# Attention with a row filter and a mixture of experts: a row index moved to the scalar engine, a small copy moved to GpSimd, and second buffers for finished rows

## The chip, the cores and the metric

The kernel runs on one core of a Trainium2 chip. The metric is the device time of one execution in microseconds (us), lower is better. The core's engines run their own instruction queues in order and meet through semaphores: the tensor engine (PE; its weight loads are PEld), the vector engine (DVE), the scalar engine (ACT), GpSimd (POOL) and the sync engine (SP), which only issues DMAs here. POOL issues the indirect DMAs, those whose row addresses lie in a tile.

## The reference

Eight batches of eight heads, 576 rows, head width 64, all float32. Attention keeps, for each row, the scores that reach its 32nd largest; the result is the input of a mixture of eight experts in which each of the 4608 tokens goes to the expert of its largest logit.

```python
scores = scale * np.matmul(q, k.transpose(0, 1, 3, 2))
kth = np.partition(scores, -top_k, axis=-1)[..., -top_k:-top_k + 1]
scores = np.where(scores >= kth, scores, -1000000000.0)
attn = np.exp(scores - np.max(scores, axis=-1, keepdims=True))
x = (attn / (np.sum(attn, axis=-1, keepdims=True) + 1e-09)) @ v     # then [B*S, H*D]
logits = x @ w_gate; expert_idx = np.argmax(logits, axis=1)
out[mask] = gate_w[mask, None] * (np.maximum(x[mask] @ w1[e], 0.0) @ w2[e])
```

## The kernel before

**Steps and batches.** The attention part is one Python loop over 144 steps `t` (18 to a batch, 9 to a group `n` of four heads). A step owns a pair of 128-row score tiles. In the instruction order of step `t` stand: on ACT the exponential of step t-4 (`exps`, L451), the signs of step t-2 (`softmax`, L429) and the copies of the scores of step t+3 out of PSUM (L356, L375); on PE the score matmuls of t+3 (L354), the products with v of step t-5 (L460), the transposes of step t-3 (L446); on POOL the masking of step t-2 (L430) and the small tile `nb` of step t-1 (L990); on DVE the search for the 32 largest of step t (`topk`: 21 maxima over chunks, L988, then rounds of maxima and replacements, L994). Seven pairs of score tiles rotate, so an engine can run some steps ahead of another.

**Jobs.** All other work is written as Python generators (`j_...`) that advance between steps. A `yield need(...)` ends a segment and says what the next one needs; `advance` runs at most one segment of each job after a step, as long as its sums of needs stay under `LIMITS`. What a segment puts in the POOL queue is issued at once behind the step (`gq`); what it puts in the PE, ACT and DVE queues (`pq`, `aq`, `dq`) is issued inside the next step, the DVE part between the instructions of L994. All of these have line L252 in the profile. After the 144 steps `advance` is called without limits, and then in `drain`, one round between two pieces of the expert part.

- `j_rows(n)` scales the finished rows into `xm`, `xl` and the parts of their logits into `lp`, `lpl` (DVE), and SP stores these.
- `j_find(b)` finds up to 128 rows of batch b whose filter has to be done again. It makes their numbers `li` (copied by ACT from PSUM), joins both columns to an index `fl`, and lets POOL gather by it: `r_at`, `r_nb`, a segment later `r_sb`.
- `j_redo(b)` filters these rows anew; it begins when `j_find(b)` has ended (`FOUND`), and starts `j_patch(b)`, whose first segment may run only at positions 1 to 5 of a group of nine (`FREE`), as long as steps last.
- `j_route(b)` finds the expert of each token. `hist` holds a running count in column `KB` and the batch's one-hot columns behind it; a windowed sum gives `cum`, whose last column is the new running count. It is read by the next batch's sum, and by a matmul in two batches and once at the end.

**Expert part.** Weights come in pieces, are split in two parts by ACT, DVE and POOL (L919 to L922), and feed three matmuls for each product (L1107, L1122). Five smaller units of work on tokens of early batches begin before all tokens are routed; their rows are gathered by POOL (`gx`, L841), three gathers just ahead of their transposes (L1087).

Of the kernel before, what the change touches and what calls it, by code (L numbers as in the profile page):

```python
# [8 lines left out]
F32 = mybir.dt.float32  # L9
F32R = mybir.dt.float32r  # L10
BF = mybir.dt.bfloat16
I32 = mybir.dt.int32
I8 = mybir.dt.int8
AF = mybir.ActivationFunctionType
OP = mybir.AluOpType
# [32 lines left out]
def attention_moe(ctx, tc, q, k, v, w_gate, w1, w2, out):  # L48
# [214 lines left out]
    def need(**k):  # L263
        return k
# [249 lines left out]
    def j_rows(n):  # L514
        b = 2 * n // HP

        xm = jobs.tile([128, 2 * MAIN, 128], F32, name="xm", bufs=1)
        xl = jobs.tile([128, 128], F32, name="xl", bufs=1)
        lp = jobs.tile([128, 2 * MAIN, 2 * E], F32, name="lp", bufs=1)
        ll_ = jobs.tile([128, 2 * E], F32, name="lpl", bufs=1)  # L520
        pts = {}

        def turned(m):
            pt = pts[m] = bank()
            for c in range(3 * m, min(3 * m + 3, 2 * MAIN)):
                i, g = divmod(c, 2)
                pe(nc.tensor.matmul, pt[:, (c - 3 * m) * RW:(c - 3 * m + 1) * RW], XT[2 * n + g][:, i * 128:(i + 1) * 128],
                   turner[:, (2 * n + g) % HP], start=True, stop=True)

        def scaled(x, l, pt, r):  # L530
            w = pt.shape[1] // RW
            v = pt.rearrange("p (c x) -> p c x", x=RW)
            vec(nc.vector.tensor_tensor, x.rearrange("p c (h d) -> p c h d", h=2),
                v[:, :, 0:128].rearrange("p c (h d) -> p c h d", h=2), r.to_broadcast([128, w, 2, D]), op=OP.mult)
            vec(nc.vector.tensor_tensor, l.rearrange("p c (h e) -> p c h e", h=2),
                v[:, :, 128:].rearrange("p c (h e) -> p c h e", h=2), r.to_broadcast([128, w, 2, E]), op=OP.mult)

        def done(m):
            c = slice(3 * m, min(3 * m + 3, 2 * MAIN))
            w = c.stop - c.start  # L540
            r = RI[n][0].rearrange("p i g h -> p (i g) h")[:, c, :, None]
            scaled(xm[:, c], lp[:, c], pts[m][:, 0:w * RW], r)

        yield need(bank=1, pe=0.75)
        turned(0)
        while n not in RI:
            yield
        for m in range(2):
            yield need(bank=1, pe=0.75 if m == 0 else 1.1, dve=0.6)
            done(m)  # L550
            vec(release, pts[m])
            turned(m + 1)
        pt = pts[2]
        o = 2 * RW
        for g in range(2):
            r = slice(g * LEFT, (g + 1) * LEFT)
            pe(nc.tensor.matmul, pt[r, o:o + RW], XT[2 * n + g][:, 512:S], turner[:, (2 * n + g) % HP], start=True, stop=True)
        for h in range(2):
            for g in range(2):
                r = slice(g * LEFT, (g + 1) * LEFT)  # L560
                pe(nc.tensor.matmul, pt[r, o + RW + h:o + RW + h + 1], ident[:, h * LEFT:(h + 1) * LEFT],
                   RI[n][1][:, g:g + 1], start=True, stop=True)
        yield need(dve=1.0)
        done(2)
        rl = jobs.tile([128, 2], F32, name="rl")
        vec(nc.vector.tensor_copy, rl, pt[:, o + RW:o + RW + 2])
        scaled(xl[:, None], ll_[:, None], pt[:, o:o + RW], rl[:, None, :, None])
        vec(release, pt)
        yield
        yield  # L570
        t0 = PAD + b * S
        for dst, x, l in ((xs, xm, xl), (lps, lp, ll_)):
            w = dst.shape[1] // 4
            f = slice((n % 2) * 2 * w, (n % 2 + 1) * 2 * w)
            nc.sync.dma_start(dst[t0:t0 + M, f].rearrange("(p i) f -> p i f", p=128),
                              x.rearrange("p (i g) f -> p i (g f)", g=2))
            for g in range(2):
                nc.sync.dma_start(dst[t0 + M:t0 + S, f.start + g * w:f.start + (g + 1) * w], l[g * LEFT:(g + 1) * LEFT])
        STORED.add(n)
# [8 lines left out]
    def j_find(b):  # L588
        sm = lambda name, shape, dt=F32: jobs.tile(shape, dt, name=name, bufs=1)
        yield need(dve=0.3)  # L590
        key = sm("r_key", [128, NLT])
        vec(nc.vector.scalar_tensor_tensor, key, CNT[b], float(2 * TOPK - S), idx1, op0=OP.not_equal, op1=OP.mult)
        vec(nc.vector.max, rhs[:, :, 0], key)
        ok = sm("r_ok", [128, 9], BF)
        vec(nc.vector.tensor_scalar, ok[:, 0:8], rhs[:, :, 0], 0.0, None, op0=OP.is_gt, op1=OP.add,
            accum_out=ok[:, 8:9])
        nbb = NBB[b % 2]
        ntab = dram.tile([128 * (NLT + 1), 2], F32, name=f"ntab{b}")
        nc.sync.dma_start(ntab.rearrange("(p t) a -> p t a", p=128), nbb)
        yield need(spot=1, pe=0.1)  # L600
        pr, leave = spot("stat")
        pe(nc.tensor.matmul, pr[:, 0:1], before, ok[:, 8:9], start=True, stop=True)
        pe(nc.tensor.matmul, pr[:, 1:3], ones, ok[:, 7:9], start=True, stop=True)
        act(nc.scalar.activation, stat[:, b], pr[:, 0:3], AF.Copy)
        act(leave)
        yield need(slack=1)
        yield need(dve=1.3)
        sl = sm("r_sl", [128, 8], BF)
        vec(nc.vector.scalar_tensor_tensor, sl, slots[:, 0:8], stat[:, b, 0:1], ok[:, 0:8], op0=OP.add, op1=OP.mult)
        oh = sm("r_qx", [128, 512]).bitcast(BF).rearrange("p (j x) -> p j x", j=8)  # L610
        vec(nc.vector.tensor_tensor, oh, slots[:, None, :].to_broadcast([128, 8, 128]),
            sl[:, :, None].to_broadcast([128, 8, 128]), op=OP.is_equal)
        yield need(spot=1, pe=0.5)
        pl, leave = spot("li")
        for j in range(8):
            pe(nc.tensor.matmul, pl[:, 0:2], oh[:, j], rhs[:, j], start=(j == 0), stop=(j == 7))
        li = sm("r_li", [128, 2])
        act(nc.scalar.activation, li, pl[:, 0:2], AF.Copy)
        act(leave)
        yield need(slack=1)  # L620
        yield need(dve=0.1)
        fl = sm("r_fl", [128, 1], I32)
        vec(nc.vector.scalar_tensor_tensor, fl, li[:, 1:2], float(NLT + 1), li[:, 0:1], op0=OP.mult, op1=OP.add)
        yield need(pool=2.0)
        at = sm("r_at", [128, 4], I32)
        pool(nc.gpsimd.indirect_dma_start, out=at, out_offset=None, in_=atab,
             in_offset=bass.IndirectOffsetOnAxis(ap=fl[:, 0:1], axis=0))
        nb = jobs.tile([128, 8], F32, name="r_nb", bufs=3)
        pool(nc.gpsimd.indirect_dma_start, out=nb[:, 0:2], out_offset=None, in_=ntab,
             in_offset=bass.IndirectOffsetOnAxis(ap=fl[:, 0:1], axis=0))  # L630
        yield need(pool=1.8)
        qi = jobs.tile([128, 2], I32, name="r_qi", bufs=3)
        pool(nc.gpsimd.tensor_scalar, qi, at[:, 0:3:2], b * H * S, None, op0=OP.add)
        sb = jobs.tile([128, S], F32, name="r_sb", bufs=2)
        pool(nc.gpsimd.indirect_dma_start, out=sb, out_offset=None, in_=SCD[b],
             in_offset=bass.IndirectOffsetOnAxis(ap=at[:, 0:1], axis=0))
        hf = sm("r_hf", [128, 1])
        pool(nc.gpsimd.tensor_copy, hf, at[:, 1:2])
        hm = jobs.tile([128, H], F32, name="r_hm", bufs=3)
        pool(nc.gpsimd.tensor_scalar, hm, eight, hf, None, op0=OP.is_equal)  # L640
        hmb = hm[:, :, None].to_broadcast([128, H, D])
        pool(nc.gpsimd.tensor_scalar, used[:, b:b + 1], hf, float(H), None, op0=OP.is_lt)
        yield need(pool=0.7)

        low = nb[:, 2:3]
        pool(nc.gpsimd.tensor_scalar, nb[:, 3:4], nb[:, 1:2], 1.0 + 2.0 ** -10, None, op0=OP.mult)
        pool(nc.gpsimd.tensor_scalar, low, nb[:, 0:1], -(2.0 ** -7), None, op0=OP.mult)
        pool(nc.gpsimd.tensor_tensor, low, low, nb[:, 3:4], op=OP.add)
        FOUND[b] = (sb, nb, qi, hmb)
# [106 lines left out]
    def j_route(b):  # L756
# [26 lines left out]
        vec(nc.vector.tensor_tensor, hist[:, :, KB + 1:].rearrange("p e c -> p c e"), oh, valid, op=OP.mult)  # L783
        win = bass.AP(hist.tensor, hist.offset, [list(hist.ap[0]), list(hist.ap[1]), [1, KB + 1], [1, KB + 1]])
        vec(nc.vector.tensor_reduce, cum, win, axis=AX.X, op=OP.add)
        vec(nc.vector.tensor_copy, hist[:, :, KB], cum[:, :, KB])
        yield need(spot=1, pe=0.1, act=0.2)
        act(nc.scalar.activation, ex, sh, AF.Exp)
        rk, leave = spot("rank")
# [5 lines left out]
        act(leave)  # L795
        yield need(slack=1)
        yield need(dve=0.7)
        sm = small("gsm", [128, KB])
        pool(nc.gpsimd.iota, pay[:, :, 3:4], pattern=[[0, KB], [0, 1]], base=0, channel_multiplier=0)
        pos = small("pos", [128, KB], I32)  # L800
# [641 lines left out]
```

## Time and profile before

| | |
|---|---|
| median of 3 runs | 1323.11 us (1320.73 to 1324.79) |
| the profiled execution: its own time, its span | 1327.61 us, 1325.8 us |
| granted clock of the tensor engine, mean | 0.985 |
| busy share of the span: PE, DVE, ACT, POOL | 95%, 78%, 62%, 68% |
| the chain that ended last, by engine | PE 62%, DVE 19%, issue 6%, POOL 5%, ACT 5% |
| attention steps | about 12 to 790 us, a batch about 98 us from the third on |
| 1100 to 1200 us (expert part): PE, DVE busy | 100.00, 37.83 us |

A busy share says how long an engine executed anything, held-up instructions included. The chain is followed back from the last instruction, at each step to what released it or to the instruction before it on its engine; "issue" is time for which the profile shows no cause. Times in a timeline are start, then duration.

### The profile page before, as it was taken

What the parts mean: (1) busy time and instruction counts of PE and PEld (TensorE: products, weight loads), DVE (VectorE), ACT (ScalarE), POOL (GpSimd) and SP (SyncE); (2) the same over time, 40 slices, a digit from 0 to 9 for tenths busy, and PEclk for the clock granted to TensorE, in tenths of its full rate; (3) what the DMA queues carried; (4) which work ended last, traced back from release to release, by engine and by line L of the source; (5) the groups of instructions that cost most, each with busy time, mean ns of one, the idle gap of its engine ahead of it and who ended that gap; (6) DMA issues with size and microseconds to landing.
All of it is one profiled execution on the core that took longest, in us unless ns stands there. A gap on an engine that the chain in (4) does not pass through costs nothing.

```text
span 1325.8 us, 32793 instructions
## 1 busy us (share of the span) xinstructions
PE 1265.1 (95%) x9688; PEld 1007.6 (76%) x9688; DVE 1037.6 (78%) x6838; ACT 823.2 (62%) x1691; POOL 905.2 (68%) x1272
## 2 busy tenths in 40 slices
PE   5999999999999999999999988998999999999997
PEld 3677777777677777777676767888799898989996
DVE  6999999999999999999998985745673333345664
ACT  3998898888788788788887863433233323233442
POOL 3777886887887887888877886754654333245654
PEclk8999999999999999999999997999999999999999
DMA  6656564664655655555654434735654333246774
GB/s 169 202 161 175 172 206 142 174 187 147 174 173 162 169 166 161 170 167 162 173 164 134 150 119 113 221 91 159 157 178 154 109 109 115 88 151 189 219 218 124
DMA packets 271244, 211.25 MB, mean 159 GB/s; under 512 B 136216, under 2 KB 214216, under 8 KB 271056
## 3 DMA queue, kind: packets, MB, share of 16 engines
q1 hardware_dynamic: 260320, 185.92, 48.3%
q0 software_dynamic: 9504, 22.86, 5.4%
q8 instruction: 78, 1.28, 0.4%
q14 instruction: 110, 0.90, 0.2%
q10 hardware_dynamic: 1232, 0.30, 0.1%
HBM read 102.49 MB, written 107.90 MB: 159 GB/s over the span
## 4 chain that ended last, share of the span: by engine, by line
PE 62%; DVE 19%; issue 6%; POOL 5%; ACT 5%; DMA 2%; SPq 1%; POOLq 0%; ACTq 0%; DVEq 0%
PE ph L1107 16%; PE y L1122 15%; DVE cand L988 9%; PE ps L354 6%; PE px L460 6%; PE pt L252 5%; PE tt L446 5%; DVE cand L994 3%; DVE vq L994 3%; PE tt L443 3%; PE px L475 2%; ACT sg L429 2%; POOL sb L430 2%; PE mt L1087 1%; PE px L367 1%
## 5 line engine op out<-in xcount | busy, mean ns | idle before, releaser
L430 POOL TENSOR_TENSOR sb<-sb,sg 128x576 f32<-128x576 f32 x288 | 369.8, 1292 | 133.8 <-ACT sg L429 131.1
L988 DVE MAX8 cand<-sb 128x8 f32<-128x52 f32 (+2 forms) x3024 | 368.9, 211 | 2.8 <-ACT sb L356 2.2
L922 POOL TENSOR_TENSOR wl<-r,wh 128x512 fp32r<-128x512 f32 x110 | 142.4, 1296 | 221.2 <-DVE wh L921 211.8
L429 ACT ACTIVATE sg<-sb,nb 128x576 int8<-128x576 f32 x288 | 223.1, 775 | 23.6 <-POOL nb L990 21.5
L460 PEld LDWEIGHTS px<-et,rv 128*64 128x64 f32 x2688 | 132.1, 138 | 122.6 <-issue 57.5
L1108 ACT ACTIVATE hh<-ph 128x320 fp32r<-128x320 f32 (+3 forms) x136 | 58.3, 428 | 240.8 <-PE ph L1107 218.1
L994 DVE MAX8 vq<-cand 128x8 f32<-128x22 f32 (+7 forms) x1152 | 205.2, 207 | 0.8 <-DVE cand L994 0.8
L451 ACT ACTIVATE et<-tt 128x1152 f32<-128x1152 f32 x144 | 163.1, 1132 | 44.3 <-PE tt L446 43.5
L354 PE MATMUL ps<-qk 64*128 64x512 f32 (+1 forms) x576 | 183.9, 646 | 3.1 <-ACT sb L356 2.5
L1109 DVE SCALAR_TENSOR_TENSOR hl<-ph,hh 128x320 fp32r<-128x320 f32 (+3 forms) x136 | 65.1, 479 | 149.9 <-ACT hh L1108 128.9
L460 PE MATMUL px<-et,rv 128*64 128x128 f32 (+1 forms) x2688 | 166.7, 268 | 14.8 <-ACT xt L252 4.7
L356 ACT ACTIVATE sb<-ps 128x1024 f32<-128x1024 f32 x144 | 147.0, 1020 | 51.1 <-PE ps L354 48.1
L1107 PE MATMUL ph<-xh,wh 128*128 128x320 f32 (+3 forms) x536 | 168.3, 314 | 0.0
L446 PE MATMUL tt<-turner,sb 128*128 128x128 f32 x1296 | 166.5, 273 | 0.6 <-POOL sb L430 0.6
L1107 PE MATMUL ph<-xh,wl 128*128 128x320 f32 (+3 forms) x536 | 165.0, 308 | 0.0
L1107 PE MATMUL ph<-xl,wh 128*128 128x320 f32 (+3 forms) x536 | 164.7, 307 | 0.0
L994 DVE MATCH_REPLACE8 cand<-vq,cand 128x22 f32<-128x22 f32 (+2 forms) x864 | 157.8, 190 | 0.0
L446 PEld LDWEIGHTS tt<-turner,sb 128*128 128x128 f32 x1296 | 139.4, 141 | 1.0 <-POOL sb L430 1.0
L1122 PE MATMUL y<-wh,hh 128*128 128x512 f32 x324 | 128.2, 396 | 1.3 <-ACT yo L1126 1.3
L1122 PE MATMUL y<-wh,hl 128*128 128x512 f32 x324 | 128.4, 396 | 0.0
L1122 PE MATMUL y<-wl,hh 128*128 128x512 f32 x324 | 128.2, 396 | 0.0
L1107 PEld LDWEIGHTS ph<-xh,wh 128*128 128x128 f32 x536 | 101.2, 189 | 3.5 <-issue 0.6
(245 smaller groups left out, 2398.2 us busy)
## 6 DMA issues: line engine op xcount, KB each, us to landing
r<-in_moe_w_dram SPq DMA_DIRECT2D x220, 256.0 KB
sc<-sb SPq DMA_DIRECT2D x128, 288.0 KB
sc<-sb SPq DMA_DIRECT2D x128, 256.0 KB
rv<-in_v_dram SPq DMA_DIRECT2D x32, 256.0 KB
xs<-xm SPq DMA_DIRECT2D x16, 512.0 KB
rq<-in_q_dram SPq DMA_DIRECT2D x60, 128.0 KB
rk<-in_k_dram SPq DMA_DIRECT2D x60, 128.0 KB
sc<-sb SPq DMA_DIRECT2D x32, 144.0 KB
```

The lines of the kernel that those rows point to most:

```text
L354: nc.tensor.matmul(MAINS[:, n], qk[:, 0, w], qk[:, 1, 2 * LEFT:], start=True, stop=True)
L356: nc.scalar.activation(bass.AP(EX[-1].tensor, EX[-1].offset, [list(EX[-1].ap[0]), [S + LEFT, 2], [1, M]]), MAINS, AF.Copy)
L429: nc.scalar.activation(upper(SG[i]), SB[u], AF.Sign, bias=nb[:, i, 1:2], accum_out=CNT[b][:, 2 * lt + i:2 * lt + i + 1])
L430: nc.gpsimd.tensor_tensor(SB[u], SB[u], SG[i], op=OP.add)
L446: nc.tensor.matmul(tt[:, c], x[:, c * 128:(c + 1) * 128], ident, start=False, stop=c in (3, 7, 8), is_transpose=True)
L451: nc.scalar.activation(ET[t], three.rearrange("p (c q) -> p c q", c=NB9), AF.Exp, scale=0.125)
L460: yield lambda kb=kb, blk=blk: nc.tensor.matmul(px[h * 64:(h + 1) * 64], block(rv, p % 2, kb if kb < MAIN else MAIN + n, h), et[:, blk, q] ...
L922: (nc.gpsimd if i else nc.vector).tensor_tensor(lo, r, hi, op=OP.subtract)
L988: one[m][0](*one[m][1])
L994: f(*a)
L1107: nc.tensor.matmul(ph, a[:, c, :], x[:, c, s], start=(m == 0), stop=(m == len(seq) - 1))
L1122: nc.tensor.matmul(PY[u, t], a[:, s], x, start=(f == 0 and m == 0), stop=(f == FC - 1 and m == 2))
```

## The change

`xm`, `xl`, `lp` and `lpl` get two buffers each instead of one. In `j_find`, the index `fl` is computed by ACT right behind its copy of `li` and in the same segment; the segment that held the DVE instruction is gone, so `j_find` has one segment less. In `j_route`, the copy of the running count moves from DVE, right behind the sum, to POOL, two segments later.

```diff
-        xm = jobs.tile([128, 2 * MAIN, 128], F32, name="xm", bufs=1)
-        xl = jobs.tile([128, 128], F32, name="xl", bufs=1)
-        lp = jobs.tile([128, 2 * MAIN, 2 * E], F32, name="lp", bufs=1)
-        ll_ = jobs.tile([128, 2 * E], F32, name="lpl", bufs=1)
+        xm = jobs.tile([128, 2 * MAIN, 128], F32, name="xm", bufs=2)
+        xl = jobs.tile([128, 128], F32, name="xl", bufs=2)
+        lp = jobs.tile([128, 2 * MAIN, 2 * E], F32, name="lp", bufs=2)
+        ll_ = jobs.tile([128, 2 * E], F32, name="lpl", bufs=2)
...
         act(nc.scalar.activation, li, pl[:, 0:2], AF.Copy)
         act(leave)
+        fl = sm("r_fl", [128, 1], I32)
+        act(nc.scalar.activation, fl, li[:, 1:2], AF.Identity, scale=float(NLT + 1), bias=li[:, 0:1])
         yield need(slack=1)
-        yield need(dve=0.1)
-        fl = sm("r_fl", [128, 1], I32)
-        vec(nc.vector.scalar_tensor_tensor, fl, li[:, 1:2], float(NLT + 1), li[:, 0:1], op0=OP.mult, op1=OP.add)
         yield need(pool=2.0)
...
         vec(nc.vector.tensor_reduce, cum, win, axis=AX.X, op=OP.add)
-        vec(nc.vector.tensor_copy, hist[:, :, KB], cum[:, :, KB])
         yield need(spot=1, pe=0.1, act=0.2)
...
         yield need(slack=1)
         yield need(dve=0.7)
+        pool(nc.gpsimd.tensor_copy, hist[:, :, KB], cum[:, :, KB])
```

## Rows read from the trace of the kernel before

**Rows 1.** Busy us (instructions): PE, PEld, DVE, ACT, POOL; clock, DMA share, GB/s.

```profile
300.00:400.00 100.00, 97.16 (x885) 72.19 (x882) 99.97 (x811) 83.86 (x175) 83.31 (x121) 1.00 0.56 165
```

**Rows 2.** Groups by line and shape, whole run: busy us, mean ns | idle before.

```profile
L252 DVE SCALAR_TENSOR_TENSOR r_fl<-r_li 128x1 int32<-128x1 f32 x8 | 11.3, 1407 | 0.0
...
L252 DVE COPY hist<-cum 128x8 bf16<-128x8 bf16 x8 | 5.9, 740 | 0.1
...
L990 POOL TENSOR_TENSOR nb<-vq,factors 128x4 f32<-128x4 f32 x144 | 28.4, 197 | 4.8 <-DVE vq L994 4.8
...
L252 POOL TENSOR_SCALAR r_hm<-eight,r_hf 128x8 f32<-128x8 f32 x8 | 2.6, 322 | 0.8
...
L252 ACT ACTIVATE sg<-r_sb,r_nb 128x576 int8<-128x576 f32 x8 | 6.2, 780 | 0.0
...
L252 ACT ACTIVATE r_li<-pt 128x2 f32<-128x2 f32 x8 | 1.4, 172 | 1.3 <-PE pt L252 1.3
...
L252 ACT ACT_TABLE_LOAD x1 | 1.3, 1283 | 4.0 <-DMA rk<-in_k_dram 4.0
```

**Rows 3.** Tiles r_fl and hist by stretch: ns min/median/max, first and last start.

```profile
L252 DVE SCALAR_TENSOR_TENSOR r_fl<-r_li x2: 143/146/148, 144.0 to 234.3; 128x1 int32<-128x1 f32 x2
...
L252 DVE SCALAR_TENSOR_TENSOR r_fl<-r_li x1: 2364/2364/2364, 333.1 to 333.1; 128x1 int32<-128x1 f32 x1
...
L252 DVE COPY hist<-cum x1: 1064/1064/1064, 390.8 to 390.8; 128x8 bf16<-128x8 bf16 x1
```

**Rows 4.** Timeline about 333 us: start, duration.

```profile
332.89 2.52 POOL L430 TENSOR_TENSOR sb<-sb,sg 128x576 f32<-128x576 f32 x2
...
333.07 2.36 DVE L252 SCALAR_TENSOR_TENSOR r_fl<-r_li 128x1 int32<-128x1 f32 x1
```

**Rows 5.** The chain that ended last, about 431 us: start, duration.

```profile
431.14 2.19 issue
```

**Rows 6.** Waits of DVE and of ACT, 200 to 700 us: total, times, longest.

```profile
DVE xm L252 <- PE pt L252: 0.5, 1, 0.5
DVE cand L988 <- issue: 0.3, 2, 0.2
...
ACT et L451 <- PE tt L446: 30.6, 36, 1.2
```

**Rows 7.** Timeline of ACT and DVE: score copies and the maxima that read them.

```profile
267.64 1.01 ACT L356 ACTIVATE sb<-ps 128x1024 f32<-128x1024 f32 x1
...
270.76 0.34 DVE L988 MAX8 cand<-sb 128x8 f32<-128x52 f32 x2
...
278.61 1.00 ACT L356 ACTIVATE sb<-ps 128x1024 f32<-128x1024 f32 x1
...
287.50 0.22 DVE L988 MAX8 cand<-sb 128x8 f32<-128x52 f32 x1
...
365.51 1.01 ACT L356 ACTIVATE sb<-ps 128x1024 f32<-128x1024 f32 x1
...
371.18 0.23 DVE L988 MAX8 cand<-sb 128x8 f32<-128x52 f32 x1
...
376.61 1.00 ACT L356 ACTIVATE sb<-ps 128x1024 f32<-128x1024 f32 x1
...
385.50 0.22 DVE L988 MAX8 cand<-sb 128x8 f32<-128x52 f32 x1
```

**Rows 8.** Timeline of DVE: one instruction of the redo job in two batches.

```profile
275.23 1.21 DVE L252 TENSOR_TENSOR r_v<-r_v 128x8 f32<-128x8 f32 x1
...
375.73 0.15 DVE L252 TENSOR_TENSOR r_v<-r_v 128x8 f32<-128x8 f32 x1
```

**Rows 9.** Timeline of the first expert unit: POOL's gathers and a transpose.

```profile
819.71 1.07 POOL L841 DMA_INDIRECT gx<-xs,ids  x1 [0.16 <-issue]
...
824.05 0.94 POOL L252 DMA_INDIRECT r_at<-atab,r_fl  x1 [0.31 <-issue]
...
824.81 0.60 PE L1087 MATMUL mt<-turner,gx 128*128 128x128 f32 x4
```

## What I expect the change to do, and why

> **What bounds the kernel now.** I read the busy time by stretches first. In the attention steps three engines look full: the vector engine is busy 99.97 of 100 us, the tensor engine 97.16, with ACT and POOL near 84 [rows 1]. So the question for this change, which takes work off the vector engine there, is whether its fullness sets the pace or only follows it.
>
> Second, the groups by line. The two instructions that leave the vector engine are tiny (one element and eight elements a partition) and yet cost 1407 and 740 ns on the mean [rows 2]. By stretch they are two-valued: `r_fl` took 0.15 us in the first two batches and 2.36 us at 333 us; four in a row, up to 627 us, lie between 2.33 and 2.36, of which one stands. The copy took 1.06 us at 390.8, and five like it stand between 293 and 685 us [rows 3]. The timeline says what the long ones do: POOL's pair of masking operations ends at 332.89 + 2.52 = 335.41, and `r_fl`, begun at 333.07, ends at 335.43 [rows 4]. So the instruction is held until POOL is done, and counts as busy meanwhile. Of the 99.97 us part is waiting, and the change removes two such waits a batch.
>
> Third, the chain of waits. It runs over the vector engine in every second batch, and there the stall is on it as 2.19 us of "issue" at 431.14 [rows 5]. Read alone, this says that the stall is paid for.
>
> Fourth, the hand-overs, which say the opposite. From 200 to 700 us the vector engine waited 0.8 us in all for anything, none of it for scores [rows 6], and in the whole run POOL's `nb`, the only reader of its result that starts the next stage, waited for it once, 4.8 us [rows 2]. If neither side waits for the other, there is stock on both sides. Its size can be read: a score copy and the maxima that read it are the same-numbered ones of 144. The 71st copy ends at 366.52 and its maxima begin at 371.18: 4.66 us of stock [rows 7]. The path that does wait is ACT and PE: ACT's exponential waits for the transposes 36 times, 30.6 us [rows 6], and PE waits for that exponential in its turn. I take this ring of PE, ACT and (where its jobs pile up) POOL as what sets the pace.
>
> The rows hold a test of that. In the batch before 287 us `r_fl` took 0.15 us, in the next 2.36. So the vector engine should be over 2 us earlier at the end of the first, and it is: the 53rd step begins 270.76 - 268.65 = 2.11 us after its scores, the 71st, one batch on, 4.66. Two steps later both stand at 7.89 us (287.50 - 279.61 and 385.50 - 377.61) [rows 7]. The lead of 2.55 us is gone in two steps. Where it went is seen in the redo job's little product: 1.21 us in the early batch, 0.15 in the other [rows 8]: arriving earlier, it ran into POOL's operations. A stall taken out at one place comes back at the next.
>
> **The change part by part.**
>
> *The index leaves DVE.* Eight instructions, 11.3 us [rows 2]. Four of about 2.35 (9.4 us) and two of 0.15 lie before 700 us, 1.6 us behind. By the test above the 9.4 us are worth nothing in the time; the lower end of their value is nothing, the upper 9.7. Of the last 1.6 us, when stock runs out as the steps end and the rounds of the expert part begin, I take 1.
>
> *The index on ACT.* Eight instructions that the trace does not have. Nearest: ACT's copy of two columns, 0.17 us, which stands right in front [rows 2]. From below 0.17, no gain being possible for ACT; from above 0.17 plus two reloads of the function table at 1.28 each, 2.74 us, if Identity needed another table than its neighbours. I take 0.2, since four kinds of function run here on one load [rows 2], 1.6 us in all, covered by the about 0.85 us that ACT waits each time for the transposes (30.6 over 36); without cover it costs the 1.6 us, and behind it stand the copy `xt` and the exponential, on which PE waits. On the loads, the Trainium skill, "ScalarE: Activation LUTs", section "Table sets: the hidden batching unit", says that cheap functions, identity among them, are in every set; the trace has no Identity to show it; by it no reload comes, without it the sum would be about 20 us higher.
>
> *One segment less in `j_find`.* Per batch, POOL's gathers `r_at`, `r_nb`, then `r_qi` to `used` with the gather `r_sb`, then three small operations move one step earlier, past one `nb` and, from the fourth batch on, one scatter of `j_route` in POOL's queue. SP's queue isn't touched. `j_redo` moves one step earlier too: ACT's Sign (0.78 us [rows 2]), its DVE part, POOL's subtraction, two more ACT passes. `j_patch` does not follow while steps last: its first segment waits for positions 1 to 5, and it now asks at position 8. So within a batch the same work is shuffled by a step, at no sum; from below I give it -0.5 us a batch (POOL's queue is free earlier), from above +1 (the Sign lands whole on the path). I take 0.
>
> *The copy on POOL.* Bounds: `nb`, 0.20 us for 4 elements, and `r_hm`, 0.32 for 8 [rows 2]. Eight of 0.2 to 0.32, at most 2.6 us. It reads a sum finished steps before, so it waits for nothing; behind it stand the payload's iota and the scatters. POOL has about 17 idle us in 100 [rows 1]; I take 0. The 5.9 us that leave DVE [rows 2], five of 1.07 in the steps, are like the first part worth 0 to 5.9; I take 0, by the same test.
>
> *Two buffers.* With one, the scaling could wait for the previous group's store. Its only wait in this stretch is 0.5 us, once, for PE [rows 6]; the store is nine steps old by then. Worth 0, from both sides: no instruction is added.
>
> *The sum.* -1 for the last two indices, all else 0. The profiled execution took 1327.6 us and would take 1326.6. It was 4.5 us (0.34%) slower than the median run, and I carry that over: 1323.1 - 1 = **1322 us**.
>
> **The rivals.**
>
> *A. The vector engine sets the pace.* For: 99.97 of 100 us [rows 1], and the chain [rows 5]. Then all that leaves it before 700 us counts: 9.7 + 5.3 = 15 us, and the time is 1308. If only what the chain holds counts (2.2 us for the index and about 1 for the copy, in two batches), it is 6.4 us less: 1316.7. Against: 4.66 us of stock, and the lead lost in two steps [rows 7]. The Trainium skill, "Perfetto Trace Analysis", section "Identifying the Most-Contended Engine", says to take the engine of highest occupancy as the one to improve, and that for the vector engine occupancy is a fair measure; by it this rival holds and the time is 1308. The trace agrees with the occupancy and not with the conclusion, since part of it is held-up time [rows 4]. Chances: 0.08 for the whole, 0.12 for the chain's part.
>
> *B. The redo's Sign lands on the path (slower).* ACT runs it one step earlier, in front of an exponential and the signs that POOL's masking reads. If the 0.78 us and a wait behind it, by my estimate 1 us, stay on that path in each of seven batches, 7 us: 1329. It is slower by over 0.3% from 0.7 us a batch. For: it is as long as ACT's waits (0.85 us); against: the place that it leaves gains the same. Chance 0.12.
>
> *C. POOL's queue in the first expert rounds (slower).* The last batch's two gathers now stand a round earlier. Today `gx` is issued at 819.71, `r_at` at 824.05, and the transpose that needs `gx` runs at 824.81 [rows 9]. Ahead of `gx`, they put it back by two gathers and what stands around them, 2 x (0.94 + 0.2), 2.3 us, and by as much PE if it has no reserve; as other scatters move out of the way of later gathers, I price it from +1 up to two such places, 4 to 5: up to 1327. Chance 0.06.
>
> *D. Less meeting of DVE and POOL.* POOL too is held up by two-operand work of DVE; with other positions 0.5 to 1 us a batch could be saved: 1316 to 1319. Chance 0.08.
>
> **How the numbers follow.** The forecast, no change that can be measured, has 0.54; a difference below 0.3% (4 us) is what this measurement can't tell from none. Its own range is 1318 to 1326. Faster by more: A's two parts and D, 0.28. Slower by more: B and C, 0.18. A reaches to 1308 and B to 1329; leaving out the end of either, the range is 1310 to 1328.
>
> **What would show it.** Right: the long `r_fl` is gone, a DVE instruction with two inputs at the steps just behind it or at the batch's end is longer instead, a batch of steps stays near 98 us, and the stock at the 71st step is 2 to 3 us smaller (1.5 if the copy's lead lasts till there). Wrong by A: the batch shrinks to 95 or 96 us with no new long instruction. Wrong by B: ACT's exponentials start later behind the Sign, by steps that add up to more than 98 us. A table load in front of each Identity would show the reload.

## The result: the changed kernel is slower by 1.35%

The median went from 1323.17 us (1320.73 to 1324.79) to **1341.58 us** (1338.27 to 1342.12); the ratio is 1.0135, with a 95% interval of [1.0112, 1.0158]. The time lies above the forecast's range. The profiled execution of the changed kernel took 1341.07 us with a span of 1339.2 us, 13.4 us above the span before. The medians are 18.4 us apart; most of the other 5 us are the 4.4 us by which the profiled execution of the kernel before was slower than its median run.

**Where the time went.** First the busy time by stretches of the changed kernel: the stretch of [rows 1], then two that hold the end of the steps and the first expert units.

```profile
300.00:400.00 100.00, 97.39 (x888) 71.58 (x887) 97.70 (x816) 84.27 (x176) 82.32 (x120) 1.00 0.58 167
...
800.00:820.00 20.00, 10.43 (x73) 9.47 (x74) 6.45 (x12) 4.25 (x10) 11.96 (x19) 0.74 0.34 94
820.00:860.00 40.00, 28.87 (x165) 24.11 (x165) 22.36 (x52) 11.53 (x24) 22.32 (x33) 0.87 0.49 144
```

The last two in the kernel before:

```profile
800.00:820.00 20.00, 14.37 (x88) 12.79 (x89) 11.94 (x21) 7.53 (x15) 10.85 (x14) 0.66 0.43 115
820.00:860.00 40.00, 38.73 (x236) 34.35 (x235) 28.98 (x62) 16.46 (x35) 32.40 (x46) 1.00 0.71 209
```

In the steps the vector engine now has 2.3 us of rest in 100, where it had none, and the tensor engine is no slower. The loss is in 60 us behind the steps: there the tensor engine is busy for 39.30 us instead of 53.10, 13.8 us less, about the whole difference of the spans. From 960 us on both run without a pause (340.00 of 340 us from 960 to 1300).

**The steps themselves.** The groups by line show the moved instructions, the timeline shows the same exponential of two batches that follow each other, and the hand-over at the 71st and 73rd steps as in [rows 7].

```profile
L252 ACT ACTIVATE r_fl<-r_li 128x1 int32<-128x1 f32 x8 | 2.4, 295 | 0.3
L252 POOL COPY hist<-cum 128x8 bf16<-128x8 bf16 x8 | 1.9, 234 | 0.0
```

```profile
363.61 1.03 ACT L356 ACTIVATE sb<-ps 128x1024 f32<-128x1024 f32 x1
368.06 2.56 DVE L987 MAX8 cand<-sb 128x8 f32<-128x52 f32 x21
374.19 1.00 ACT L356 ACTIVATE sb<-ps 128x1024 f32<-128x1024 f32 x1
379.97 2.56 DVE L987 MAX8 cand<-sb 128x8 f32<-128x52 f32 x21
407.10 1.13 ACT L451 ACTIVATE et<-tt 128x1152 f32<-128x1152 f32 x1
504.56 1.13 ACT L451 ACTIVATE et<-tt 128x1152 f32<-128x1152 f32 x1
```

A batch takes 504.56 - 407.10 = 97.46 us; in the kernel before the same two stand at 409.51 and 507.43 us, 97.92. The index costs ACT 0.295 us and brings no load of a table. The scores wait 3.42 us for the vector engine at the 71st step (4.66 before) and 4.78 at the 73rd (7.89 before), so it does come earlier, and keeps the lead. The pace hardly answers: half a microsecond a batch. And a batch's length in one execution says little of the time: with the copy alone (below, on another chip) the same batch took 96.44 us, 1.5 less than in the kernel before, and that kernel gained only 2.5 us in all.

**The end of the steps.** The last exponential starts 6.4 us earlier than before, and yet the first unit's products (L1106) start 2.0 us later and the second's 13.3 us later:

```profile
789.02 1.13 ACT L451 ACTIVATE et<-tt 128x1152 f32<-128x1152 f32 x1
795.99 1.12 ACT L451 ACTIVATE et<-tt 128x1152 f32<-128x1152 f32 x1
812.41 0.39 PE L1106 MATMUL ph<-xh,rv 128*128 128x256 f32 x1 [0.69 <-ACT xh L1087]
852.80 0.69 PE L1106 MATMUL ph<-xh,wh 128*128 128x384 f32 x1 [0.69 <-ACT xh L1087]
```

In the kernel before (their line is L1107 there):

```profile
789.92 1.12 ACT L451 ACTIVATE et<-tt 128x1152 f32<-128x1152 f32 x1
802.37 1.12 ACT L451 ACTIVATE et<-tt 128x1152 f32<-128x1152 f32 x1
810.40 0.58 PE L1107 MATMUL ph<-xh,rv 128*128 128x256 f32 x1 [0.69 <-ACT xh L1088]
839.54 0.33 PE L1107 MATMUL ph<-xh,wh 128*128 128x384 f32 x1
```

From the start of unit 1 on both kernels take the same time to the end of the span (486.4 and 486.3 us), so the loss is whole by then. Most of the 6.4 us lie between the last two exponentials, 6.97 us apart instead of 12.45: the jobs there stand in another order. What the two places below cost has to be read against that; their waits add up to more than the loss.

So there are two places. For the first, here are the waits of PE in the changed kernel (total, times, longest, from 795 to 860 us), and behind them its chain of waits, which says what is ahead of `r_xa` on POOL:

```profile
PE pt L252 <- POOL r_xa L252: 7.4, 1, 7.4
PE mt L1086 <- DVE xl L1088: 7.4, 2, 5.9
PE y L1121 <- DVE hl L1108: 2.5, 1, 2.5
```

```profile
798.72 1.26 POOL kt L921
...
800.17 1.81 POOL table L811
...
806.11 0.91 POOL table L811
...
807.85 1.00 POOL r_xa L252
...
808.90 1.12 PE pt L252 x4
810.02 0.85 PE mt L1086 x4
```

The patch job of batch 6 has its transposes of `r_xa` in PE's queue directly ahead of unit 0's (`mt`). Its product with the mask `r_hm` is on POOL behind the five scatters (`table`) of batch 5's routing job, and these begin only at 800.17 us, behind POOL's part of the first weights (`kt`, L921). In the kernel before the five stood ahead of these weights and ended at 799.44 us, and the patch job's transposes stood behind unit 0's.

The second place is the start of unit 1, in the timeline of PE of the changed kernel:

```profile
840.88 0.50 PE L1121 MATMUL y<-wh,hl 128*128 128x512 f32 x1 [2.52 <-DVE hl L1108]
...
841.93 0.60 PE L1086 MATMUL mt<-turner,gx 128*128 128x128 f32 x4
848.47 1.12 PE L1086 MATMUL mt<-turner,gx 128*128 128x128 f32 x4 [5.94 <-DVE xl L1088]
851.00 1.11 PE L1086 MATMUL mt<-turner,gx 128*128 128x128 f32 x4 [1.41 <-DVE xl L1088]
```

In the kernel before the three groups of transposes stand apart between pieces of unit 0, at 824.81 [rows 9], 829.32 and 833.48 us, and PE waits for none of them. Now they come in one go with nothing between them. They share one tile `mt`: PE fills it, ACT copies it, DVE subtracts, and only then may PE fill it again, 2.5 us a round. In the first round PE waited 5.94 us, since ACT had a copy of late weights (`wh`, at 845.39) ahead of it. The wait for `hl` belongs to neither place: ahead of `hl` on DVE stood the redo job of batch 7, from 837.41 to 840.40 us. The kernel that only lacks the segment (below) does not have this wait.

**Why they come in one go.** The rounds of jobs are decided by the program before anything runs, so the order can be printed from the program itself. A round is one call of `advance`; its banks are the free ones of the two PSUM tiles that the jobs share; "refused" is a job that found too few; the last columns are the expert part, its first piece being piece 0 of unit 0.

```
            kernel before                          changed kernel
round 154   redo(6) ends; route(5) takes a bank    patch(6) takes the last bank; route(5) refused
round 158   route(5) takes a bank and ends         route(5) passes its plain yield
            piece 0                                piece 0
round 159   piece 1, gather unit 1                 route(5) refused; piece 1
round 160   piece 2                                route(5) refused; piece 2
round 161   piece 3, transpose 0 of unit 1         route(5) refused; piece 3
round 162   piece 4, transpose 1 of unit 1         route(5) takes a bank and ends; piece 4, gather unit 1
round 166   unit 1                                 transposes 0, 1, 2 of unit 1, then unit 1
```

With one segment less in `j_find`, batch 6's redo ends in round 153, the last round within the steps, instead of 154. Its patch job may begin in 154, because the gate `FREE` holds only while steps last. There it meets batch 5's routing job. Both are due at the same number (18 * 8 + 12), the patch lane stands first, and one bank is free. So the routing job loses one round, and by that its last segment comes when the expert part has begun: in round 159 the rows job of the last group (`j_rows`) and the patch job, which are due earlier or stand first, take both banks, and in 160 and 161 the rows job takes the only free one. One round lost has become four.

### The profile page after: what moved, and what is told of

The parts are those of the page before. It is cut to its first block, busy times and chain, and to the rows that moved or that the text cites. A ratio compares the mean times of both kernels' runs of the same rounds, so it can differ in the third digit from the quotient of the medians.

```text
span 1339.2 us, 32779 instructions
## 1 busy us (share of the span) xinstructions
PE 1264.2 (94%) x9688; PEld 1005.8 (75%) x9688; DVE 1023.5 (76%) x6822; ACT 823.9 (62%) x1699; POOL 900.6 (67%) x1280
## 4 chain that ended last, share of the span: by engine, by line
PE 57%; POOL 13%; ACT 9%; issue 8%; DVE 6%; DMA 4%; SPq 2%; POOLq 0%; ACTq 0%; DVEq 0%
PE ph L1106 16%; PE y L1121 15%; POOL sb L430 6%; PE ps L354 5%; PE pt L252 5%; PE px L460 5%; PE tt L446 5%; ACT sg L429 3%; ACT sb L356 3%; DVE cand L987 2%; PE tt L443 2%; POOL table L811 2%; DMA sc<-sb 2%; PE px L475 2%; PE mt L1086 1%
## 5 line engine op out<-in xcount | busy, mean ns | idle before, releaser
L921 POOL TENSOR_TENSOR wl<-r,wh 128x512 fp32r<-128x512 f32 x110 | 142.3, 1295 | 239.0 <-DVE wh L920 235.7
L1107 ACT ACTIVATE hh<-ph 128x320 fp32r<-128x320 f32 (+3 forms) x136 | 58.2, 428 | 250.4 <-PE ph L1106 248.9
L1106 PE MATMUL ph<-xh,wh 128*128 128x320 f32 (+3 forms) x536 | 169.8, 317 | 1.0 <-ACT xh L1087 0.7
L460 PE MATMUL px<-et,rv 128*64 128x128 f32 (+1 forms) x2688 | 163.1, 267 | 5.0 <-ACT xt L252 2.9
L1106 PE MATMUL ph<-xh,wl 128*128 128x320 f32 (+3 forms) x536 | 166.0, 310 | 0.2 <-DVE wl L921 0.2
L1106 PE MATMUL ph<-xl,wh 128*128 128x320 f32 (+3 forms) x536 | 166.0, 310 | 0.0
L1106 PEld LDWEIGHTS ph<-xh,wh 128*128 128x128 f32 x536 | 102.1, 190 | 7.1 <-issue 2.4
```

Source lines behind the costliest of these rows:

```text
L460: yield lambda kb=kb, blk=blk: nc.tensor.matmul(px[h * 64:(h + 1) * 64], block(rv, p % 2, kb if kb < MAIN else MAIN + n, h), et[:, blk, q] ...
L921: (nc.gpsimd if i else nc.vector).tensor_tensor(lo, r, hi, op=OP.subtract)
L1106: nc.tensor.matmul(ph, a[:, c, :], x[:, c, s], start=(m == 0), stop=(m == len(seq) - 1))
```

## The experiments

All ratios are to the kernel before, run beside the changed one on the same chip. In the four sets of runs it took 1325.60, 1321.76, 1325.91 and 1325.78 us (medians of 21, 20, 29 and 9 runs; the second set was on a chip on which the kernel before is some 4 us faster). The ratios and intervals are worked out from all runs of a set; the quotient of the two medians differs from them by up to 0.13%, so differences of 0.1 or 0.2% between two ratios are to be read with care.

| kernel | median us | ratio | 95% interval |
|---|---|---|---|
| whole change, segment kept | 1324.28 | 0.9982 | [0.9971, 0.9994] |
| before, one segment less | 1343.50 | 1.0125 | [1.0110, 1.0141] |
| whole change, patch(6) waits a round | 1326.31 | 1.0011 | [0.9998, 1.0025] |
| before, unit 1's gathers 3 rounds later | 1334.54 | 1.0061 | [1.0047, 1.0075] |
| whole change, routing due first | 1327.24 | 1.0045 | [1.0031, 1.0058] |
| before, 23 us more of DVE work | 1355.11 | 1.0261 | [1.0246, 1.0276] |
| index on ACT only | 1320.24 | 0.9994 | [0.9985, 1.0003] |
| copy on POOL only | 1319.18 | 0.9981 | [0.9972, 0.9991] |
| segment kept, 23 us more of DVE work | 1329.60 | 1.0030 | [1.0016, 1.0045] |
| before, the DVE work behind `r_ok` | 1358.08 | 1.0230 | [1.0202, 1.0258] |
| second buffers only | 1325.59 | 1.0000 | [0.9988, 1.0012] |
| before, gathers 1 round later | 1328.97 | 1.0021 | [1.0011, 1.0032] |
| whole change, patch(6)'s logits wait | 1332.02 | 1.0058 | [1.0044, 1.0072] |

### The segment, kept and alone

To the whole change the empty segment is given back:

```diff
         yield need(slack=1)
+        yield need(dve=0.1)
         yield need(pool=2.0)
```

> The whole change, but the empty segment (need(dve=0.1), no instruction) stays in j_find. Theory 1 (planning): the loss of the change comes from one segment less in j_find, which lets the patch job of batch 6 start one round earlier, right as the steps end, where it takes the last PSUM bank from the routing job of batch 5; that job ends four rounds later, and with it unit 1's gathers stand three rounds later. Then this kernel has none of it: 1316 to 1323 us, ratio to the kernel before 0.995 to 1.000, unit 1 begins without a pause of the tensor engine. Theory 2 (the moved instructions themselves cost: the index on ACT, the copy in POOL's queue, or the second buffers): 1337 to 1342, ratio 1.010 to 1.015.

From the kernel before one segment of `j_find` is taken:

```diff
         act(leave)
-        yield need(slack=1)
         yield need(dve=0.1)
         fl = sm("r_fl", [128, 1], I32)
```

> The kernel before, with one segment less in j_find and nothing else of the change: the idle segment ahead of the index is left out, so the index stays on DVE and comes one step earlier. After the steps idle segments are passed over, so batch 7's gathers r_at and r_nb stand where they stood; only batch 6's redo and patch come earlier. Theory 1: the loss is there in full, 1334 to 1342 us, ratio 1.009 to 1.015, with unit 1's gathers behind the fourth piece of unit 0. Theory 2: no loss, 1320 to 1326. Theory 3 (r_at and r_nb of batch 7 ahead of the gathers of gx in POOL's queue, as rival C had it): no loss, 1320 to 1326.

0.9982 and 1.0125. The segment alone makes the loss, and the whole change without it is faster than the kernel before. None of the moved instructions is to blame, and it is not the place of batch 7's gathers, which the second kernel leaves where they were.

### The bank

In the whole change `j_patch` of batch 6 waits at its beginning:

```diff
+        if b == B - 2:
+            yield
         yield need(bank=1, nook=1, pe=0.6, act=0.7, dve=0.2, at=FREE)
```

> The whole change, and the patch job of batch 6 alone waits one round. Batch 7's gathers r_at and r_nb stay a round earlier than in the kernel before. Theory 1: the bank goes to the routing job as before, 1316 to 1323 us, ratio 0.995 to 1.000. Theories 2 and 3: the loss stays, 1336 to 1342.

In the whole change the routing job is due first:

```diff
-DUE = dict(redo=4, patch=12, sums=0, rows=0, find=3, route=12)
+DUE = dict(redo=4, patch=12, sums=0, rows=0, find=3, route=11)
```

> The whole change, and the routing job is due one step earlier than the patch job (11 instead of 12), so that of two jobs that want the last bank in one round the routing job gets it. Theory 1 (planning): the loss of the change is gone, 1317 to 1324 us, ratio 0.995 to 1.001, as with the waiting patch job (1.0011). If something else than the bank held the routing job: above 1330.

1.0011, just above what was expected, and 1.0045, a miss by 0.35%. Both give most of the loss back by who gets the bank in round 154, but neither gets down to 0.9982. What they keep from the change is that batch 7's `r_at` and `r_nb` stand a round earlier. The timeline of POOL of the kernel whose patch job waits shows them ahead of unit 1's gathers, and PE's waits (810 to 960 us) a price:

```profile
812.50 1.34 POOL L252 DMA_INDIRECT r_at<-atab,r_fl  x1 [0.15 <-issue]
814.15 0.96 POOL L252 DMA_INDIRECT r_nb<-ntab,r_fl  x1 [0.30 <-issue]
...
816.62 1.20 POOL L842 DMA_INDIRECT gx<-xs,ids  x1 [0.18 <-issue]
```

```profile
PE mt L1088 <- DMA gx<-xs,ids: 7.7, 3, 5.6
```

With the segment kept, PE waits 3.6 us for `gx` in the same stretch, 4.1 us less. Of these, 1.2 are at unit 1, behind the two gathers, as the forecast's rival C had it. The larger part, 2.7, is at unit 3: there batch 7's routing job, a round earlier too, has its first instruction ahead of the gathers in POOL's queue, and that waits for a scatter:

```profile
894.31 0.24 POOL L252 IOTA pay<- 128x8 int32 x2 [2.85 <-DMA table<-pay,pos]
896.18 1.01 POOL L842 DMA_INDIRECT gx<-xs,ids  x1
...
900.73 1.09 PE L1088 MATMUL mt<-turner,gx 128*128 128x128 f32 x4 [5.55 <-DMA gx<-xs,ids]
```

The same place with the segment kept:

```profile
893.27 0.99 POOL L841 DMA_INDIRECT gx<-xs,ids  x1 [0.18 <-issue]
...
898.33 0.63 PE L1087 MATMUL mt<-turner,gx 128*128 128x128 f32 x4 [2.86 <-DMA gx<-xs,ids]
```

The two kernels' ratios are 0.29% apart (3.8 us), their medians 2.0 us; the 4.1 us of waits fit the first, and no kernel takes these waits out alone. So rival C is there as a mechanism, at two places and of about the size that it gave, under a loss several times as large. The routing-first kernel has the same waits (8.5 us in all), and its median is only 0.9 us above that of the kernel whose patch job waits (1327.24 and 1326.31). So most of the 0.34% between their ratios is the kernel before, 3.8 us faster on the chip of the second set than on that of the first; why, no trace shows.

### The two places apart

In the kernel before unit 1's gathers are put off:

```diff
-            if f:
+            if f > (3 if u == 0 else 0):
                 fetch(u + 1)
```

> The kernel before, all its jobs where they were; only unit 1's gathers are issued three rounds later (behind the fifth piece of unit 0 instead of the second), so its five groups of transposes stand in one go at its start, as in the changed kernel. If the lateness of these gathers is what costs (second half of theory 1): 10 to 15 us more, 1333 to 1338, ratio 1.008 to 1.012. If the loss is in the weights' loads or in the other order of the jobs: 1321 to 1326.

In the whole change `j_patch` of batch 6 waits ahead of its logits:

```diff
+        if b == B - 2:
+            yield
         yield need(spot=1, pe=0.2, act=0.1, pool=1.4)
         pl, leave = spot("logit")
```

> The whole change, and the patch job of batch 6 waits one round just ahead of its logits, so that the routing job of batch 5 gets its last bank one round after the steps and unit 1's gathers stand where they stood. The patch job's transposes of r_xa stay ahead of unit 0's on PE, and the five scatters stay ahead of r_xa on POOL. If the loss has two places, each with its own price (the start of unit 0, the late gathers of unit 1): the first stays, 5 to 9 us above the kernel with the segment kept, 1325 to 1332 us where the kernel before takes 1323, ratio 1.002 to 1.006, and PE waits 5 to 8 us for r_xa. If the late gathers are the whole loss: ratio 0.997 to 0.999. If the start of unit 0 is the whole: 1.010 to 1.013.

In the kernel before the gathers are put off by one round only:

```diff
-            if f:
+            if f > (1 if u == 0 else 0):
                 fetch(u + 1)
```

> The kernel before with unit 1's gathers one round later instead of three (behind the third piece of unit 0), the transposes where they were. If the price of late gathers follows the time by which they come too late: the first lands about a round (3 us) later, and the transposes of unit 1 begin in the next round, so 0 to 4 us more, ratio 1.000 to 1.003. If any lateness costs the whole: 8 us more, ratio 1.006.

Late gathers alone cost 0.61%, less than expected, and the first place alone 0.58%, as expected. The second kernel also carries the waits of rival C (0.29%) and the 0.18% that the rest of the change gained; without them it is 0.47%, and the two places together 1.08%. The segment alone, which has neither, cost 1.25% (1.10 to 1.41). So the two places are the loss nearly or wholly, and some 0.2%, about what the intervals leave open, is not assigned. Each kernel has its own wait of PE and not the other's (795 to 860 us). Gathers three rounds late:

```profile
PE mt L1087 <- DVE xl L1089: 6.2, 2, 4.8
```

The patch job's logits a round later, with the gathers on time:

```profile
PE pt L252 <- POOL r_xa L252: 7.4, 1, 7.4
```

One round of lateness costs 0.21%, a third of what three rounds cost: in these two runs the price follows the number of rounds, though PE then waits for `gx` itself (2.4 us) and not for `mt`.

### The parts, and more work for the vector engine

Each part alone on the kernel before: the index with its segments kept, the copy, and (not shown) `bufs=2` for the four tiles:

```diff
         act(leave)
+        fl = sm("r_fl", [128, 1], I32)
+        act(nc.scalar.activation, fl, li[:, 1:2], AF.Identity, scale=float(NLT + 1), bias=li[:, 0:1])
         yield need(slack=1)
         yield need(dve=0.1)
-        fl = sm("r_fl", [128, 1], I32)
-        vec(nc.vector.scalar_tensor_tensor, fl, ...)
...
-        vec(nc.vector.tensor_copy, hist[:, :, KB], cum[:, :, KB])
...
         yield need(dve=0.7)
+        pool(nc.gpsimd.tensor_copy, hist[:, :, KB], cum[:, :, KB])
```

> Of the change only the index on ACT, with the number of segments of j_find kept, so that no job moves: the DVE instruction is gone and its segment is empty. Forecast's theory: no change that can be measured, ratio 0.997 to 1.001. Rival A: 9.7 us less, ratio 0.992 to 0.993. A reload of ACT's table at each index: 20 us more, ratio 1.015.

> Of the change only the copy of the running count on POOL. Forecast's theory: no change that can be measured, ratio 0.998 to 1.002. Rival A: 5.3 us less, ratio 0.996. If the copy in POOL's queue cost: above 1.003.

> Of the change only the second buffers. Forecast's theory: worth 0, ratio 0.998 to 1.002; it has to be above 1.008 if the buffers cause the loss, which the kernel with the segment kept already speaks against.

0.9994, 0.9981, 1.0000. Rival A is out by the first: 9.7 us less were wanted, 0.8 came (at most 2). The copy is worth 2.5 us (1.2 to 3.7), the buffers nothing that can be measured.

Ten more instructions in `j_find`: in the kernel before, in the whole change with the segment kept, and in the kernel before behind `ok` instead of ahead of it:

```diff
         vec(nc.vector.max, rhs[:, :, 0], key)
+        more = sm("r_more", [128, 8])
+        for _ in range(10):
+            vec(nc.vector.max, more, ident)
```

> The kernel before with ten more maxima on DVE in j_find, over a constant of 128 columns, result unused. By the rows of 88 columns (244 ns) and 576 (761 ns) one should take about 290 ns, an estimate: 2.9 us of real work a batch, 23 us in eight, 17 us in the six batches in which DVE is busy all the time. If DVE holds stock on both sides and does not set the pace (the forecast's theory): 0 to 3 us more, ratio 1.000 to 1.003. If DVE sets the pace (rival A): 15 to 20 us more, ratio 1.011 to 1.015.

> The ten maxima (2.84 us a batch, as measured) at the same place, but on the whole change with the segment kept. There r_ok was ready 6.0 us before PE came to it (494.15 and 500.13 us), in the kernel before 2.4 us. If the loss of 33 us was this one deadline (PE's matmul that waits for r_ok): 3.2 us of reserve are left, 0 to 6 us above the kernel before, ratio 1.000 to 1.005. If DVE's work as a whole sets the pace: 15 to 33 us above, ratio 1.011 to 1.025.

> The kernel before with the ten maxima behind r_ok instead of ahead of it, so that in its own batch the matmul does not wait for them. If the deadline of r_ok was the cause: below 10 us more, ratio under 1.008. If DVE was full already and every microsecond more counts: 17 to 33 us more, ratio 1.013 to 1.025.

The first fell outside both theories: 33 us more, for 80 instructions of 284 ns, 22.7 us. The forecast's "stock on both sides" does not hold in this direction. On the changed kernel with its segment the same work costs 0.48% (from 0.9982 to 1.0030), some 6 us. That alone would have fitted one deadline, PE's matmul that waits for `r_ok`; but behind `r_ok` the work costs the kernel before nearly as much (2.30%), so one deadline it was not. The busy time from 200 to 700 us suggests why: first the kernel before, then the changed kernel with its segment.

```profile
200.00:700.00 500.00, 487.41 (x4411) 359.45 (x4409) 498.92 (x4062) 420.10 (x873) 411.06 (x589) 1.00 0.57 167
```

```profile
200.00:700.00 500.00, 489.17 (x4437) 361.53 (x4437) 486.24 (x4088) 422.56 (x884) 410.82 (x594) 1.00 0.57 167
```

The same with the work added, in the same order, and behind the first of them PE's wait for `r_ok`, the tile `r_fl` (ns min/median/max), and PE's largest wait for DVE in the same stretch of the kernel that has the work behind `r_ok`:

```profile
200.00:700.00 500.00, 475.83 (x4235) 350.30 (x4234) 499.47 (x3953) 404.02 (x838) 399.29 (x572) 0.98 0.55 161
```

```profile
PE pt L252 <- DVE r_ok L252: 16.0, 5, 4.1
```

```profile
L252 DVE SCALAR_TENSOR_TENSOR r_fl<-r_li x5: 358/2324/2357, 239.7 to 646.3; 128x1 int32<-128x1 f32 x5
```

```profile
PE pt L252 <- DVE lp L252: 12.4, 9, 2.1
```

```profile
200.00:700.00 500.00, 488.87 (x4428) 360.32 (x4428) 499.69 (x4110) 421.38 (x878) 414.08 (x593) 1.00 0.56 167
```

With the change and its segment the vector engine rests 13.8 us in 500, some 2.7 a batch, and the 2.84 us of new work fill just that rest. In the profiled execution of the kernel before there was next to no rest (1.1 us): the new work goes past the edge, the index on DVE stays held up for 2.3 us, PE waits for the vector engine, and a microsecond of work costs 1.5. How the 4.8 us a batch (33.4 over the seven batches behind the first of these instructions) divide among these was not taken apart. Nor is it shown that the change bought this room. Kernels that still have the index on DVE show it too, in executions in which the index is not held up for the 2.3 us: with the gathers three rounds late the vector engine was busy 486.90 of 500 us, with the copy alone on POOL 487.79. What is shown is that the work cost the kernel before 33 us and the changed kernel with its segment 6.

## Why the prediction was wrong, step by step

**The step that failed** is "One segment less in `j_find`", and in it the sentence that "`j_patch` does not follow while steps last ... So within a batch the same work is shuffled by a step, at no sum". It is true of the six batches whose patch job begins within the steps, and ends with the steps. The very next round has no gate; there the patch job of batch 6 does follow, one round early. The forecast named the gate's condition and did not ask what happens in the first round in which it no longer holds. What the runs showed in its place: the patch job took the bank of batch 5's routing job, PE waited 7.4 us for `r_xa`, unit 1's gathers came three rounds late, and this step, put at no sum, cost 1.25% (16.6 us) by itself. That a moved segment changes who gets a PSUM bank was in no rival. It was to be had from the kernel alone: two jobs due at the same number, both wanting a bank, and two banks in all.

**The vector engine does not set the pace**: right as to what taking work from it gives. Rival A whole (1308 us) is out by the index alone, and the chain's part (6.4 us less) by the kernel with the segment kept, 0.8 to 3.8 us less. The Trainium skill, "Perfetto Trace Analysis", section "Identifying the Most-Contended Engine", would have taken the engine with the highest occupancy first; the runs disagree as to the gain, which is 2.4 us with all that the change takes from it. The reason given, stock on both sides that swallows any change, was wrong in the other direction: 22.7 us of added work cost 33.

**"The lead is gone in two steps"** was read from too little. In the changed kernel the lead stays (4.78 us at the 73rd step, 7.89 before), and the stall does not come back at the next place: with the segment kept the vector engine is busy 486.24 of 500 us. The time is hardly better for it. So the test's conclusion held, but not by the test's reason; what does hold the pace in the steps no run here took apart.

**The index on ACT**: 0.295 us for the 0.2 taken, and the load of the table did not come, as the Trainium skill, "ScalarE: Activation LUTs", section "Table sets: the hidden batching unit", had it (identity is in every set). **The copy**: 0.234 us, inside the bounds; for its removal from DVE 2.5 us came where 0 was taken and 5.9 was the end. **The buffers**: 0, as said.

**Rival B** (the Sign on the path) is not seen: a batch is 0.46 us shorter. **Rival C** was right as a mechanism and of about its size, 2 to 4 us, as the kernel with the waiting patch job shows; it looked at POOL's queue in the first expert rounds, and not at the banks. In the changed kernel itself it is not seen: there PE waits only 2.9 us for `gx` from 810 to 960 us, less than before (5.1). **Rival D** could not be told apart from the half microsecond a batch.

## What to carry to other kernels

When a change takes out or adds a segment in a program that plans itself, the order behind it changes wherever two jobs compete for a tile, a bank or a turn; print both orders and compare them at the ends of loops, where gates and limits change, before costing a single instruction. A stage that begins early needs its first inputs early too: three small gathers three rounds late cost 0.6%. An engine from which work can be taken without gain may still have no room for more: measure both signs, with work taken away and with work added.

## What the runs showed of the hardware that was not expected

The stall that the change was to remove is not a property of the instruction. The kernel with late gathers has the same instructions in the steps as the kernel before, and in its profiled execution the index on DVE was not held up from 200 to 700 us:

```profile
L252 DVE SCALAR_TENSOR_TENSOR r_fl<-r_li x5: 142/148/149, 232.1 to 622.2; 128x1 int32<-128x1 f32 x5
```

In the kernel before, four of the same five took 2.33 to 2.36 us. The vector engine was busy 486.90 of 500 us there instead of 498.92. Of these 12 us, 8.8 are the index and 2.2 the copy `hist` (five of 0.64 us at the median instead of 1.07). Whether an instruction is held up hangs on when it meets POOL's masking, and either phase lasted through batch after batch. A batch was no shorter for it beyond 0.2 us (97.75 and 97.95 us, between the same exponentials of two batches), which is the forecast's point once more. The Trainium skill, "SBUF — State Buffer", section "SBUF: two separate sides", says that DVE, for an instruction with two SBUF inputs or in a two-port mode, and GpSimd share a port pair that the first to start keeps for its whole instruction. [rows 4] agree with that (the index has two SBUF inputs and ends at 335.43 us, POOL's masking at 335.41), and the runs add that whether the two meet is a matter of phase.

The tensor engine's waits at unit 1 are charged twice. Four transposes behind the 5.94 us pause took 1.12 us, those before it 0.60; the granted clock was 1.00 (2.4 GHz) from 820 to 838 us, where PE was busy 17.47 of 18 us, and 0.50 (1.2 GHz) from 848 to 853 us, behind the pause. At unit 0 it is the other way round. In the kernel before PE came to unit 0 just after pauses of 4.18 and 1.26 us; the granted clock was 0.50 (1.2 GHz) from 807 to 812 us and 0.58 from 812 to 816. In the changed kernel PE had begun again at 808.90 us, and the clock was 0.98 (nearly all at 2.4 GHz) from 812 to 820. Unit 0's first products (L1107, L1106) took 5.4 us before and 3.5 now, so 1.9 us of the first place's loss came back.
